# Block-sparse attention with a following MLP: v cast on chip, masks turned by DMA, narrower bounds and a new order

## The chip, the cores and the metric

The kernel runs on one core of one Trainium2 chip. The metric is the device time in microseconds (us) of one execution, as the median of several runs of the same kernel. A profiled execution of its own gives the page and the trace that are shown; times in the profile count from the start of its span.

The names of the engines are those of the profile: PE is TensorE, PEld its weight loads, DVE is VectorE, ACT is ScalarE, POOL is GpSimd, SP is SyncE. SP here only issues DMAs. SBUF is the on-chip memory, PSUM the memory into which TensorE writes.

## The reference

There are two stages. q, k and v are fp32 of shape (4, 8, 768, 64): batch, head, position, feature. The first stage is an attention in which each query sees six chunks of 32 keys:

```
ub[s, c] = sum over d of max(q[s,d] * kmin[c,d], q[s,d] * kmax[c,d])     # kmin, kmax: over the 32 keys of chunk c
ub = where(s // 32 >= c, ub, -1e9)
chosen[s] = the 6 chunks with the largest ub[s, :]
scores = q @ k.T / 8, masked to the chosen chunks and to keys t <= s
x = softmax(scores) @ v
```

The heads are then put side by side, which gives x of shape (4, 768, 512), and the second stage is a normalised two-layer MLP with a residual:

```
xn = (x - mean(x)) / sqrt(var(x) + 1e-6) * g_ln
out = x + relu(xn @ w_ch1) @ w_ch2       # 512 -> 2048 -> 512, fp32 out
```

## The kernel before

**Tiling.** A tile has 128 positions, so a sequence has 6 tiles, in two halves of 3 (r = 0 and r = 1). Two heads go together, since two times 64 features fill 128 partitions: a group g is one batch and one pair of heads. There are 16 groups, four to a batch. Groups 0 to 3 (batch 0) are loaded and prepared in two halves, groups 4 to 15 whole.

**Steps of a group.** `ld` and `ldb` load k and q by SP's DMA queue. `turn` brings features onto partitions: on PE through PSUM for groups 0 to 3 (L218, fp32), on DVE in blocks of 32 x 32 for the others (L212). `kbound` reduces k to the minimum and maximum of each chunk (L262, L263), and `kdiag` spreads these into a block matrix (`BD`, and its two 16-bit parts `BH`). With the identity max(qm, qM) = qm + relu(q)(M - m), the upper bounds are matrix products. In groups 0 to 3 `qpos` makes two fp32 operands on ACT and `bounds` runs L309 and L313; six products that nobody reads, 240 columns wide (L306), stand ahead of them. In the other groups `qhi`, `qlo` and `qrel` split q into 16-bit parts, and `bounds` takes 20 products of 96 columns (L297): four for each of five tiles. (The first tile needs no choice.) `select` (L326 to L332, on DVE) adds the causal term, takes the 8 largest of each row and writes a row of ones where a chunk is not chosen (`MN`).

**The mask in the scores.** The operands of the score products have 128 rows, of which only 64 are features of one head. The other 64 rows carry the mask: on the side of k constant rows with -61440 where a key belongs to a chunk (`rrows`, L148 and L149, copied from a constant `RT`), on the side of q the turned `MN`. `maskt` turns it on PE (L341), and `mring` copies it from PSUM into the operands `QA` and `QB` with two DVE copies (L346, L347). `qring` brings q there and `kcopy` k (L268, L269, ACT). A product of both then gives the score with the mask in it.

**Attention.** `smm` takes the score products of up to four blocks for each of the two heads (L396) into a PSUM tile, `sexp` is the exponential on ACT (L404), `diag` clears the part above the diagonal on POOL (L411), `values` multiplies by v with a column of ones beside it (L423), and `norm` divides by that column's sum (DVE, L437). `pstat` takes statistics of x (L453).

**v.** `ldv` loads v by POOL's DMA queue, which turns fp32 into fp16 on the way (L189, L196).

**MLP.** For each batch and half: `centre` (L465, DVE), `xt` (L482, three DMA transposes on SP's queue), `m1` (L489) and `relu` (L498, ACT) in eight pairs of hidden tiles, `m2` (L511), `fin` (L520, DVE: scale, add x, store by SP). `rstd` gives the reciprocal deviation (L476, POOL). `w1` and `w2` load the weights in four pieces each, on POOL's queue; each first copies one element of `kc` into the piece (L155, L159), so that a load cannot start before that `kc` exists.

**The order.** Each engine works through its own queue in order. The order is written out: the string `ORDER` lists the steps, and the instructions of each engine, SP's and POOL's DMA issues among them, are chained as the steps come in the string. A step such as `m1.0.0.8` is batch 0, half 0, hidden tiles 8 and 9. PSUM has two pools: two tiles of two banks (tag `mm`: scores and m1) and four of one bank (tag `one`: turns, bounds, masks, values, m2). A step that takes a tile waits until the user before the last two, or the last four, is done with it. `warm` and `idle` (L357) are products that nobody reads; they keep PE occupied.

Of the kernel before, what the change touches and what calls it, by code (L numbers as in the profile page):

```python
# [9 lines left out]
ACTF = mybir.ActivationFunctionType  # L10
ALU = mybir.AluOpType
# [8 lines left out]
def kernel(  # L20
# [10 lines left out]
    nc = tc.nc  # L31
# [9 lines left out]
    VW = 72  # L41
# [36 lines left out]
    RT = const.tile([P, S], F16, name="RT", tag="RT")  # L78
    tiny = const.tile([1, 1], F32, name="tiny", tag="tiny")
    hsel = const.tile([P, 3, 2], F32, name="hsel", tag="hsel")  # L80
# [18 lines left out]
    st = [dict() for _ in range(NG)]  # L99
    hf = {}  # L100
    x_tiles = {}

    def consts():
        make_identity(nc, ident_f)
        rr = RT[0:64, :]
        nc.gpsimd.memset(rr, -NEGM)
        nc.gpsimd.affine_select(
            out=rr, in_=rr, compare_op=ALU.is_ge, fill=0.0,  # L110
            base=0, pattern=[[1, S]], channel_multiplier=-CH,
        )
        nc.gpsimd.affine_select(
            out=rr, in_=rr, compare_op=ALU.is_ge, fill=0.0,
            base=CH - 1, pattern=[[-1, S]], channel_multiplier=CH,
        )
# [7 lines left out]
        nc.vector.memset(hsel[0:64, 0, 1:2], -KS)  # L124
        nc.vector.memset(hsel[64:P, 0, 0:1], -KS)
        nc.vector.memset(hsel[0:64, 1:3, 1:2], KS)
        nc.vector.memset(hsel[64:P, 1:3, 0:1], KS)
# [18 lines left out]
    def rrows(i, r):  # L146
        c = slice(r * TR * P, (r + 1) * TR * P)
        nc.vector.tensor_copy(KA[i][64:P, c], RT[0:64, c])  # L148
        nc.vector.tensor_copy(KB[i][0:64, c], RT[0:64, c])  # L149

    def w1(j, g):
        c = slice(j * HID // 4, (j + 1) * HID // 4)
        nc.gpsimd.tensor_copy(w1b[0:1, 0, c.start:c.start + 1], st[g]["kc"][0:1, 0, 0:1])  # L155
        nc.gpsimd.dma_start(w1b[:, :, c], w1_r[:, :, c])

    def w2(j, g):
        nc.gpsimd.tensor_copy(w2b[0:1, 4 * j, 0:1], st[g]["kc"][0:1, 0, NCH // 2:NCH // 2 + 1])  # L159
        nc.gpsimd.dma_start(w2b[:, 4 * j:4 * j + 4, :], w2_r[:, 4 * j:4 * j + 4, :])  # L160

    def ld(g, i):
        b, hp = divmod(g, HP)
        both = ldp.tile([P, 2, TR, 2, D], F32, name="raw", tag="raw")
        for e, (nm, src) in enumerate((("kn", k), ("qn", q))):
            t = st[g][nm, i] = both[:, e]
            for hh in range(2):
                nc.sync.dma_start(
# [13 lines left out]
    def ldv(g, i=None):  # L182
        b, hp = divmod(g, HP)
        if not i:
            st[g]["va"] = vap.tile([P, 2, NT, VW], F16, name="va", tag="va")
            nc.gpsimd.memset(st[g]["va"][:, :, :, D:D + 1], 1.0)
        va = st[g]["va"]
        if i is None:
            nc.gpsimd.dma_start(  # L189
                va[:, :, :, 0:D].rearrange("p h t d -> p (h t) d"),  # L190
                v[b, 2 * hp:2 * hp + 2].rearrange("h (t p) d -> p (h t) d", p=P),
            )
            return
# [469 lines left out]
```

## Time and profile before

| | us |
|---|---|
| median of three runs (282.27, 282.9, 287.85) | 282.9 |
| profiled execution | 284.41 |
| its span | 282.5 |
| PE busy (2529 products) | 268.8, 95% |
| DVE busy (627 instructions) | 209.9, 74% |
| ACT busy (246) | 185.0, 65% |
| POOL busy (162) | 92.4, 33% |

The page counts as busy what an engine computes; issuing a DMA is not counted for SP, and for POOL the casting DMAs of v and of the weights appear as instructions in the timeline. PE's busy time is drawn from modelled ends, so a busy PE may still run slowly or stretched by waits. A slice is 282.5/40 = 7.06 us long. In a line of a group the columns are: line, engine, operation, out<-in, partitions x elements and type, count, busy us, mean ns. In the chain a line is start, duration and what it was.

### The profile page before, as it was taken

To read this page: it belongs to the slowest core of one execution; us is meant where nothing else is said; L and a number is where in the kernel's file an instruction comes from. 1 tells how busy PE (TensorE), PEld (TensorE's weight loads), DVE (VectorE), ACT (ScalarE), POOL (GpSimd) and SP (SyncE) were. 2 spreads that over 40 slices of the span, in tenths; PEclk is the share of its full clock that TensorE was granted. 3 is DMA by queue.
4 is the path that set the end of the run, shared out by engine and by line. 5 is a ranking of instruction groups with operands and counts; after the bars stand their busy time and mean duration, and the time that the engine had idled before them with its cause. 6 is when DMAs were issued, how large, how long until landed. Compare 5 with 4: busy or idle time off the path is not lost.

```text
span 282.5 us, 6594 instructions
## 1 busy us (share of the span) xinstructions
PE 268.8 (95%) x2529; PEld 177.8 (63%) x2529; DVE 209.9 (74%) x627; ACT 185.0 (65%) x246; POOL 92.4 (33%) x162
## 2 busy tenths in 40 slices
PE   5899699999998999999999999999999999999994
PEld 2788567677655867666666766576667745555541
DVE  6889969999999979997779899969885842301112
ACT  2889969999946867867677776776968332423320
POOL 8816335453391022607462702410254000100100
PEclk9599979999999999999999999999999999999999
DMA  6999999999999764698997667663021120500202
GB/s 140 206 192 146 212 144 138 169 166 194 151 155 182 129 141 95 89 157 164 115 142 149 127 63 83 113 117 111 0 67 39 39 56 15 152 2 37 74 2 111
DMA packets 136062, 32.41 MB, mean 115 GB/s; under 512 B 127072, under 2 KB 132960, under 8 KB 136032
## 3 DMA queue, kind: packets, MB, share of 16 engines
q1 hardware_dynamic: 106640, 24.39, 45.0%
q0 software_dynamic: 29248, 7.34, 27.5%
q8 instruction: 20, 0.33, 0.5%
q10 hardware_dynamic: 144, 0.26, 0.4%
q14 instruction: 10, 0.08, 0.1%
HBM read 27.53 MB, written 6.29 MB: 120 GB/s over the span
## 4 chain that ended last, share of the span: by engine, by line
PE 82%; DVE 6%; DMA 5%; ACT 4%; issue 1%; SPq 0%; DVEq 0%; ACTq 0%
PE yp L511 28%; PE mm L489 27%; PE mm L396 12%; PE sm L423 6%; DMA raw<-in_k_dram 4%; PE ub L297 3%; ACT pt L404 2%; PE ub L313 2%; PE tr L218 2%; PE trh L341 1%; PE idle L357 1%; DMA raw<-in_q_dram 1%; PE ub L306 1%; DVE kc L262 1%; DVE kc L263 1%
## 5 line engine op out<-in xcount | busy, mean ns | idle before, releaser
L404 ACT ACTIVATE pt<-mm 128x1024 f16<-128x1024 f32 (+2 forms) x96 | 84.5, 916 | 20.4 <-PE mm L396 19.5
L511 PE MATMUL yp<-w2b,hT 128*128 128x512 f16 (+2 forms) x400 | 92.5, 370 | 0.0
L489 PE MATMUL mm<-xT,w1b 128*128 128x384 f16 x512 | 87.8, 326 | 1.3 <-ACT hT L498 1.2
L498 ACT ACTIVATE hT<-mm 128x768 f16<-128x768 f32 x64 | 51.3, 810 | 54.1 <-PE mm L489 53.7
L489 PEld LDWEIGHTS <-w1b 128*128 128x128 f16 x512 | 49.4, 98 | 34.5 <-issue 1.6
L511 PEld LDWEIGHTS <-hT 128*128 128x128 f16 x400 | 37.5, 98 | 34.1
L411 POOL TENSOR_SCALAR_AFFINE_SELECT pt<-pt 128x768 f16<-128x768 f16 x32 | 28.1, 885 | 77.4 <-ACT pt L404 77.3
L520 DVE SCALAR_TENSOR_TENSOR ot<-yp,rstd,x 128x512 f32<-128x512 f32 (+2 forms) x25 | 17.8, 716 | 44.5 <-PE yp L511 34.8
L396 PE MATMUL mm<-QA,KA 128*128 128x128 f16 (+2 forms) x224 | 34.2, 246 | 1.4 <-ACT pt L404 0.8
L396 PE MATMUL mm<-QB,KB 128*128 128x128 f16 (+2 forms) x224 | 34.2, 246 | 0.0
L476 POOL TENSOR_TENSOR rstd<-ve,mhalf 128x3 f32<-128x3 f32 x8 | 7.0, 873 | 58.0 <-DVE ve L473 57.9
L423 PE MATMUL sm<-va,pt 128*128 128x65 f16 x672 | 25.3, 193 | 0.6 <-ACT pt L404 0.3
L423 PEld LDWEIGHTS <-pt 128*128 128x128 f16 x672 | 24.0, 98 | 2.5 <-ACT pt L404 0.4
L396 PEld LDWEIGHTS <-KA 128*128 128x128 f16 x224 | 18.1, 98 | 11.2 <-issue 2.9
L453 DVE BATCH_NORM_STATS2 bst<-x 128x6 f32<-128x128 f32 x96 | 20.3, 278 | 0.0
L396 PEld LDWEIGHTS <-KB 128*128 128x128 f16 x224 | 17.9, 98 | 3.9 <-issue 0.4
L438 DVE TENSOR_TENSOR x<-sm,rden 128x384 f32<-128x384 f32 x32 | 17.8, 557 | 1.1
L465 DVE SCALAR_TENSOR_TENSOR xc<-x,mv,gall 128x512 f16<-128x512 f32 x24 | 16.8, 756 | 0.6 <-DMA xT<-xc 0.6
L281 POOL TENSOR_TENSOR kc<-kc 128x24 f32<-128x24 f32 x12 | 6.0, 502 | 31.3 <-DVE kc L263 21.7
L346 DVE COPY QA<-trh 64x640 f16<-64x640 f16 (+2 forms) x20 | 8.6, 428 | 8.3 <-PE trh L341 7.9
L218 PE MATMUL tr<-ident_f,raw 128*128 128x128 f32 x48 | 8.9, 316 | 4.2 <-DMA raw<-in_q_dram 2.2
L189 POOL DMA_DIRECT2D va<-in_v_dram x12 | 12.7, 1060 | 0.1
(85 smaller groups left out, 347.7 us busy)
## 6 DMA issues: line engine op xcount, KB each, us to landing
out_dram<-ot SPq DMA_DIRECT2D x23, 256.0 KB, 2.1
qnb<-in_q_dram SPq DMA_DIRECT2D x48, 96.0 KB, 3.2
knb<-in_k_dram SPq DMA_DIRECT2D x48, 96.0 KB, 3.3
va<-in_v_dram POOLq DMA_DIRECT2D x12, 192.0 KB, 5.4
w1b<-in_moe_w_ch_dram POOLq DMA_DIRECT2D x4, 512.0 KB, 8.2
w2b<-in_moe_w_ch_dram POOLq DMA_DIRECT2D x4, 512.0 KB, 7.1
raw<-in_k_dram SPq DMA_DIRECT2D x16, 96.0 KB, 4.3
raw<-in_q_dram SPq DMA_DIRECT2D x16, 96.0 KB, 4.2
```

What stands on the lines that cost most here:

```text
L218: nc.tensor.transpose(pst[:, t * P:(t + 1) * P], src[:, t], ident_f)
L396: nc.tensor.matmul(sc[:, hh, o:o + w * P], ks[:, t * P:(t + 1) * P], qs[:, s * P:(s + w) * P], start=True, stop=True,)
L404: nc.scalar.activation(st[g]["pt", r][:, 4 * i:4 * i + o].rearrange("p n h x -> p h n x"), st[g]["sc", r, i][:, :, 0:o * P].rearrange("p h ...
L411: nc.gpsimd.affine_select(out=dv, in_=dv, compare_op=ALU.is_ge, fill=0.0, base=0, pattern=[[0, 2 * TR], [1, P]], channel_multiplier=-1,)
L423: nc.tensor.matmul(pv[:, hh, s2, :], pt[:, where[t, s], hh, :], va[:, hh, t, 0:D + 1], start=(t == 0), stop=(t == s),)
L438: nc.vector.tensor_tensor(xh(b, r)[:, :, 2 * hp:2 * hp + 2, :].rearrange("p s h d -> p h s d"), pv[:, :, :, 0:D], rden.to_broadcast([P, 2, ...
L453: nc.vector.bn_stats(half(b, r)["st"][:, i, hp], xh(b, r)[:, i, 2 * hp:2 * hp + 2].rearrange("p h d -> p (h d)"),)
L465: nc.vector.scalar_tensor_tensor(h["xc"][:, i, :], xs, h["mv"][:, i, 0:1], gall, op0=ALU.subtract, op1=ALU.mult,)
L489: nc.tensor.matmul(hp_[:, i, 0:TR * P], w1b[:, kt, (m + i) * P:(m + i + 1) * P], h["xT"][:, kt], start=(kt == 0), stop=(kt == KT1 - 1),)
L498: nc.scalar.activation(h["hT"][:, m:m + 2], h["hp", m][:, :, 0:TR * P], ACTF.Relu, scale=HS)
L511: nc.tensor.matmul(h["yp", i][:, cs], h["hT"][:, kt, i * P:(i + 1) * P], w2b[:, kt, cs], start=(kt == 0), stop=(kt == KT2 - 1),)
L520: nc.vector.scalar_tensor_tensor(ot[:, cs], h["yp", i][:, cs], h["rstd"][:, i:i + 1], xh(b, r)[:, i].rearrange("p h d -> p (h d)")[:, cs], ...
```

## The change

- **v.** `ldv` loads fp32 by SP's queue into a buffer `vr` (two of them), and a new step `vcast` copies it as fp16 into `va`: on POOL (22 of 32 steps), ACT (5) or DVE (5). SP gets 40 DMAs for it.
- **Masks of groups 4 to 15.** `maskt` is a DMA transpose on SP's queue, from SBUF to SBUF, into one buffer; `mring` copies from there, on POOL (8) or DVE (4).
- **Bounds of groups 4 to 15.** Three of the four products of a tile take only the chunks that the tile can see: 32, 48, 64, 80 or 96 columns.
- **First x.** For batch 0, half 0, `xt` turns on PE (12 products), and a new step `xe` copies the result from PSUM.
- **Start.** q of groups 0 and 1 is loaded by ACT's queue; k of group 1 and of group 0 come first, and the load of g_ln (`gall`) comes after them. `RT` is gone: `rrows` multiplies a broadcast part of the identity by -61440. In groups 0 to 3 a new step `qcopy` makes one scaled fp32 copy of q (`q32`), from which `qpos` makes `r32` and `qring` the rows of `QA` and `QB`; `kdiag` takes the difference of maximum and minimum there too.
- **Weights.** The copies of one element are gone; w1.0, w1.1, w1.2, w1.3 and then the four pieces of w2 stand in `ORDER` after `vcast.1.1`, `vcast.2.1`, `diag.0.1` and `qring.3.1`.
- **Engines.** A step may be written `step@n`: n picks the engine from a list. So `kcopy` of the later groups is 11 times on POOL, `relu` 11 times on DVE, `qhi` 7 times on DVE, `norm` 5 times on ACT, `rrows` 3 times on ACT, `kdiag` of groups 0 to 3 6 times on POOL.
- **Fill products.** For steps on PE, n picks how many unread products stand ahead (`busy`): 8 to 32 of 122 or 128 columns, 4 to 16 of 240, 2 to 8 of 512. The six ahead of `bounds` and the separate `idle` steps are gone.
- **Order.** `ORDER` is another string from its first step to near its last.

The diff's core (`ORDER` only by its places around the weights):

```diff
+    fill = {P: (8, 16, 32), 240: (4, 8, 16), 512: (2, 4, 8), 122: (8, 16, 32)}
+    def pick(*engines):
+        return engines[min(other[0], len(engines) - 1)]
...
     def rrows(i, r):
-        nc.vector.tensor_copy(KA[i][64:P, c], RT[0:64, c])
-        nc.vector.tensor_copy(KB[i][0:64, c], RT[0:64, c])
+        for t, o in ((KA[i], 64), (KB[i], 0)):
+            scaled(
+                pick(nc.vector, nc.scalar),
+                t[o:o + 64, r * TR * P:(r + 1) * TR * P].rearrange("p (c e) -> p c e", e=CH),
+                ident_f[o:o + 64, o + c.start:o + c.stop].unsqueeze(2).to_broadcast([64, n, CH]), -NEGM,
+            )
...
-    def w1(j, g):
+    def w1(j):
         c = slice(j * HID // 4, (j + 1) * HID // 4)
-        nc.gpsimd.tensor_copy(w1b[0:1, 0, c.start:c.start + 1], st[g]["kc"][0:1, 0, 0:1])
         nc.gpsimd.dma_start(w1b[:, :, c], w1_r[:, :, c])
...
+            queue = nc.scalar if (i, nm) == (0, "qn") and g < 2 else nc.sync
...
-    def ldv(g, i=None):
-            nc.gpsimd.dma_start(
-                va[:, :, :, 0:D].rearrange("p h t d -> p (h t) d"),
-                v[b, 2 * hp:2 * hp + 2].rearrange("h (t p) d -> p (h t) d", p=P),
-            )
+    def ldv(g, i):
+        t = st[g]["vr", i] = ldp.tile([P, NT, D], F32, name="vr", tag="vr", bufs=2)
+        if g >= HP:
+            nc.sync.dma_start(t, v[b, 2 * hp + i].rearrange("(t p) d -> p t d", p=P))
+            return
...
+    def vcast(g, i):
+        eng = pick(nc.gpsimd, nc.scalar, nc.vector)
+        if g >= HP:
+            copy(eng, va[:, i, :, 0:D], t)
...
+    def busy(o, n=None):
+        w = o.shape[1]
+        for _ in range((0, *fill[w])[other[0]] if n is None else n):
+            nc.tensor.matmul(o, MN[0][:, 0, :], MN[0].rearrange("p s c -> p (s c)")[:, 0:w], start=True, stop=True)
...
     def kcopy(g, i=None):
-        nc.scalar.copy(KA[g % NK][0:64, a * P:z * P], kt[0:64, :])
-        nc.scalar.copy(KB[g % NK][64:P, a * P:z * P], kt[64:P, :])
+        eng = pick(nc.scalar, nc.vector) if g < HP else pick(nc.scalar, nc.gpsimd, nc.vector)
+        copy(eng, KA[g % NK][0:64, a * P:z * P], kt[0:64, :])
+        copy(eng, KB[g % NK][64:P, a * P:z * P], kt[64:P, :])
...
     def bounds(...):
+                    w = NCH if e == 0 else (s + 1) * P // CH
                     nc.tensor.matmul(
-                        ub[:, s - 1].rearrange("p l h c -> p (l h c)"), st[g][nm][:, s * P:(s + 1) * P],
-                        BH[g % NB][:, arr].rearrange("p l h c -> p (l h c)"), start=(e == 0), stop=(e == 3),
+                        ub[:, s - 1, :, :, 0:w], st[g][nm][:, s * P:(s + 1) * P],
+                        BH[g % NB][:, arr, :, :, 0:w], start=(e == 0), stop=(e == 3),
                     )
...
     def maskt(g, i=None):
+        if g >= HP:
+            pm = prp.tile([P, NT - 1, P], F16, name="mT", tag="mT", bufs=1)
+            nc.sync.dma_start_transpose(pm, st[g]["mn"].rearrange("p s c -> p (s c)"))
+            return
...
     def xt(b, r, i):
+        if (b, r) == (0, 0):
+            pst = h["xp", i] = ps_t.tile([P, KT1, P], F16, name="xtr", tag="one")
+            for kt in range(KT1):
+                nc.tensor.transpose(pst[:, kt], h["xc"][:, i, kt * P:(kt + 1) * P], ident_h)
+            return
...
     ORDER
-        ... sexp.2.0.0 w1.2.3 w1.1.3 w1.0.2 ld.3.1 ...
+        ... vcast.1.1 ldv.2.1 w1.0 vcast.2.1 ...
+        ... xe.0.0.0 w1.1 ldv.3.1 ... qring.4 w1.2 w1.3 kdiag.3.1@1 ...
+        ... m1.0.0.0 turn.5.qn turn.5.kn relu.0.0.0@1 w2.2 ... m1.0.0.2 w2.0 ... w2.3 rrows.2.1@1 w2.1 ...
```

## The prediction

> **What bounds the kernel now.** I read the page's slices first, then ten-microsecond windows, the chain of waits, a stretch of the timeline and the groups by shape. Slices:
>
> ```profile
> PE   5899699999998999999999999999999999999994
> DVE  6889969999999979997779899969885842301112
> PEclk9599979999999999999999999999999999999999
> ```
>
> PE is full from slice 14 (92 us) to the end; its gaps and the two drops of the clock (5 and 7) lie in the first 40 us. Windows (time; busy and count of PE, PEld, DVE, ACT, POOL; clock; DMA; GB/s):
>
> ```profile
> 0.00:10.00 10.00, 5.99 (x24) 3.23 (x25) 7.12 (x29) 4.33 (x9) 9.12 (x22) 0.91 0.90 157
> 10.00:20.00 10.00, 9.61 (x72) 8.63 (x70) 7.84 (x33) 8.12 (x20) 2.94 (x4) 0.75 1.56 210
> ...
> 80.00:90.00 10.00, 8.82 (x55) 4.91 (x54) 9.96 (x12) 5.08 (x7) 6.13 (x12) 1.00 1.46 178
> ...
> 100.00:110.00 10.00, 10.00 (x126) 7.01 (x125) 7.70 (x23) 8.02 (x10) 3.42 (x4) 1.00 0.60 125
> ```
>
> DVE's nine windows before 90 us are busy 7.12, 7.84, 9.38, 8.97, 8.68, 9.80, 9.69, 9.85 and 9.96: 8.7 us short, 5.0 of it before 20 us. At 100 us that has turned: PE 10.00, DVE 7.70. The chain has the same hand-over:
>
> ```profile
> 0.80 4.78 DMA raw<-in_k_dram
> ...
> 29.83 5.59 DMA raw<-in_k_dram
> 36.43 2.13 PE idle L357 x5
> ...
> 80.23 1.50 DVE q L235
> 83.08 1.48 DVE r L242
> ...
> 120.34 11.72 PE mm L489 x72
> ```
>
> A k load waits at the start and another at 30 us; DVE ends last around 80 us; after 92 us only PE does. L235 and L242 cost 1.5 us there. The timeline of DVE and POOL tells why:
>
> ```profile
> 80.12 0.92 POOL L411 TENSOR_SCALAR_AFFINE_SELECT pt<-pt 128x768 f16<-128x768 f16 x1
> 80.23 1.50 DVE L235 SCALAR_TENSOR_TENSOR q<-qnT,q 128x640 f16<-128x640 f32 x1
> 81.66 1.50 DVE L241 TENSOR_SCALAR r<-q 128x640 f16<-128x640 f16 x1
> ```
>
> L241 takes 0.31 us where POOL is idle. L332, L235, L241 and L242 lose 3.3 us in that stretch, some 6.5 in the whole head.
>
> So the span is a sum: DVE's work up to the hand-over, DVE's idle time and latencies, PE's work after it, the tail. Before: DVE's instructions ahead of fin.0.0.1, for whose PSUM slot bounds.7 waits, come to 80.7 us; idle 8.7; semaphores and the first product 1.9; PE's own work is 252.7 in all (below), 65.7 of it ahead of bounds.7, so 187.0 remains; after the last matmul (278.4) 4.1. Together 282.4, and the span is 282.5.
>
> PE's own work takes rates from the chain where PE isn't waiting: 512 columns 216 ns (0.86 for 4), 384 columns 162 (1.30 for 8), 96 columns 42.5 (0.85 for 20), 65 columns 30.3 (0.91 for 30), 128 columns 56 (0.45 for 8). Times counts: m2 83.0 (368 of 512, 16 of 384 and 16 of 128 columns), m1 83.2 (512), scores 37.0 (448 of three widths), values 20.4 (672), bounds 10.2 (240), masks 4.5 (80), the turns and bounds of batch 0 14.1, small ones 0.3.
>
> **What the Trainium skill says.** "SBUF — State Buffer", Who interferes with whom: VectorE and GpSimd share an SBUF port pair under an exclusive lock. The trace agrees (1.50 against 0.31 us, above). "DMA: Bandwidth & Descriptors", SWDGE vs HWDGE vs iDMA: a cast within a DMA needs the GpSimd queue, so v on SP must be fp32 and cast afterwards. The trace has the old form alone. "TensorE: Matmul & The Clock Gate", Part 1: The HAM clock gate: too little work halves TensorE's clock. It agrees: clock 0.75 in 10 to 20 us, and a fill of 512 columns takes 426 ns there, 216 later.
>
> **The change part by part.**
>
> *PE.* Masks: 60 of 80 turns go, ×56 ns = −3.4. Narrower bounds: three of four products of a tile drop from 96 columns to 32, 48, 64, 80, 96; by the 65-column rate the first three cost 30 and the fourth 36, so a group saves 3×(3×12.2+6.5) = 0.13 us, and twelve 1.5; between 0 and 2.4 if a narrow product costs no less, or falls in proportion. I take 2.0. First x on PE: 12×56 = +0.7. Total 248.0. Fills grow from 33 to 114 products, 9.6 us; they stand ahead of products that wait, so I cost them at nothing. Where nothing waits, each is PE time, 2 to 3 us if a quarter is misplaced.
>
> *DVE up to the hand-over.* The same tally over the new order says values.5.1, which waits for the slot of select.7, hands over: one select more than before. Less: rrows 3 of 8 on ACT and cheaper −2.8, later mask copies on POOL or at SBUF price −2.4, early ones on ACT −2.0, kdiag −0.8, constants −0.5. More: the extra select 2.2, kcopy 2×0.93, relu 2×0.86 (L498's tile, priced as the reduce of 768 fp32), qhi 3×0.5 ("VectorE: DVE Perf Modes", The perf-mode tier table: fp32 from SBUF runs at 2×; 0.86 if it doesn't), qrel 1.2, qlo 0.8, xT copies 2×0.43, qring 0.6, pstat 0.6, qpos 0.5, norm 0.2. Net +3.6: 84.3. By then PE has done 70.7; 177.5 remain. The extra select costs 2.2 but moves 5 us of PE work before the hand-over.
>
> *DVE idle.* The first k and q: the 256 KB of gall no longer ahead, q on ACT's queue: about 1 us earlier. The wait at 30 us: ld.3.1's issue on SP took 3.86 us beside three 512 KB weight loads and landed 5.6 later; now it precedes them: 1.5 less. Idle 6.2, latency 1.9.
>
> *POOL and the lock.* Up to the hand-over POOL's computing goes from 26.8 to about 50 us. By the slope between a CAST of 96 elements (264 ns) and an affine of 768 (865): vcast 9×0.52 = 4.7, kcopy 4×2×0.87 = 7.0, mring 2×2×0.75 = 3.0, qring 4×2×0.52 = 4.2, kdiag some 4.4. POOL loses in exchange the issue of v (1.0 us a piece). The lock cost 6.5 us for 26.8 of POOL's, but only where a fast DVE form meets it; selects, reduces, transposes and statistics show no effect. In proportion +6, at nothing 0; I take 2 and keep −1 (fewer DMA writes by POOL) to +6.
>
> *v, masks and SP's queue.* SP gets 40 v DMAs and 12 mask transposes, loses 3 xT and 4 q. At 0.53 us (median issue) and 1.2 (xT) that is +32 us on 155; SP was issuing 19 of each 20 us at first, so ldb, xt and qring behind it are late by what it waits. Those are issued two groups ahead. A later mask is now SP 1.2, landing 2.5, POOL 1.5 in place of PE 0.28, DVE 0.98: some 4 us longer; by PE's tally its scores stand over 5 us further on, so I cost it at nothing; without that distance it is up to 4 us once, since later ones overlap. With one mT buffer a maskt also waits on SP for the mring before it, and behind it stand ldb, xt, qring and the stores; xt is what PE's m1 waits for. On POOL a vcast waits for v's landing (3 to 4 us), and behind it stand diag, for which values waits, kdiag and the weights. Both are covered while PE has other work ahead; DVE's idle term would grow otherwise.
>
> *Weights.* Without the artificial wait eight 512 KB loads run back to back on POOL's queue, 3.3 us apart as the three before (28.3, 31.2, 34.8). I place w1.0's issue at 36 and the columns that m1.0.0.8 needs at 49, where PE wants them at 47.6; such a wait of up to 3.5 us is absorbed, since DVE hands over later. ACT gives up relus and copies and stays under its tally.
>
> **Sum.** 84.3 + 6.2 + 1.9 + 2.0 + 177.5 + 4.1 = 276.0 against the span of 282.5. The profiled execution is 284.4 (1.9 around the span), 1.5 above the median of 282.9; I carry the difference of −6.5 to the median: 276.4.
>
> **Rivals.**
>
> *The lock takes it.* POOL's work coincides with qlo, qrel and the selects as at 80 us: 6 to 7 instead of 2, 281. For: 23 us more work. Against: much of it falls on unaffected operations.
>
> *PE becomes the bound sooner.* DVE's idle falls by 3 and the lock by 2 below my terms: 271. For: fills keep the clock up and ACT takes DVE's copies. Against: DVE's idle of before was mostly loads, which the change only brings forward by 2.5.
>
> *Weights late (slower).* PE is in order: while m1.0.0.8 waits, nothing behind it runs. The span is then 276.0 + (landing − 47.6 − 3.5); it passes that of before once the third w1 piece lands after 57.6. For: the burst shares DMA with SP's new v loads, and a w1 piece took 8.2 us from issue to landing in the median. If pieces come one after another at that, w1.0 lands at 43 and the third at 59.4: 284.3, in the median 284.7. Against: three overlapped before.
>
> *The change isn't what it says.* v stays fp32 in HBM, so the same bytes are read and twice as many written on the chip; if the DMA engines bind in the head (their column reads 1.56 at 10 to 20 us), moving v to another queue brings nothing and costs the casts. The loads would then land no earlier, idle would stay at 8.7, and the sum is 278.5, within the first case.
>
> **Numbers.** As summed: 0.57 (273.5 to 279). Lock: 0.20 (279 to 283). PE sooner: 0.13 (269 to 273.5). Late weights or SP: 0.10 (283 to 291). Leaving out the ends, 270 to 284. Two per cent, which is about what a measurement of this kernel can tell, is 277.2 and 288.6: of the first case 0.43, with 0.13, is faster: 0.56; slower 0.05; the rest within.
>
> **What would show it.** DVE at 9.7 or more up to about 95 us; the last DVE piece of the chain near 94; chain pieces of 20 products of L297's successor near 0.7 us instead of 0.85; no `trh` of 640 columns; L411 and the new POOL casts beside 1.5-us DVE instructions if the lock counts; no gap ahead of m1.0.0.8. I am wrong if PE has a gap at L489 in the first batch, if SP's queue holds xt or qring, or if PE's last gap comes before 85 us.

## The result, and the profile after

The changed kernel takes 286.62 us in the median (four runs, 286.13 to 287.56); the kernel before takes 283.25 us in the median of its four runs (282.27 to 287.85). Executions more than 1.5% above the fastest of the same kernel, such as the one of 287.85, count as slow and are left out of every ratio given here. The ratio is 1.0134, with a 95% interval of 1.0086 to 1.0182: 1.3% slower, where 2.3% faster was forecast (276.4 us, range 270 to 284). How much slower is less certain than that interval says, since only three executions of the kernel before stand in it: measured again beside the experiments below, its median was 285.06 to 286.1 us, and 286.62 is 0.2 to 0.6% above that. No measurement shows a gain. The profiled execution took 286.18 us and its span is 284.5 us, 2.0 more than before.

The slices of the page, as shown for the kernel before:

```profile
PE   5899988996999999999999999999999999999994
DVE  7686999889799997999999899969964685321412
PEclk9856999999999999999999999999999999999999
```

PE is full from slice 11 on, as before from slice 14, but the half clock has moved: it now lies at 14 to 28 us, where PE had its full clock before. The windows (time; busy and count of PE, PEld, DVE, ACT, POOL; clock; share of the DMA engines; GB/s):

```profile
0.00:10.00 10.00, 6.80 (x46) 4.21 (x46) 7.41 (x29) 3.94 (x7) 1.51 (x9) 1.00 0.86 184
10.00:20.00 10.00, 8.99 (x53) 8.04 (x53) 6.89 (x24) 7.72 (x18) 5.52 (x17) 0.60 0.82 169
20.00:30.00 10.00, 10.00 (x103) 9.24 (x104) 6.97 (x26) 6.71 (x13) 2.73 (x8) 0.72 0.96 185
...
50.00:60.00 10.00, 9.78 (x65) 5.75 (x62) 8.68 (x28) 6.15 (x9) 3.23 (x6) 1.00 1.43 216
60.00:70.00 10.00, 7.51 (x130) 6.13 (x128) 8.75 (x27) 5.65 (x7) 4.33 (x7) 1.00 1.32 193
70.00:80.00 10.00, 10.00 (x102) 6.23 (x99) 8.36 (x23) 7.72 (x18) 6.79 (x10) 1.00 0.91 159
80.00:90.00 10.00, 10.00 (x94) 6.24 (x93) 9.90 (x23) 6.31 (x9) 5.07 (x10) 1.00 0.65 161
```

DVE is short of 30 by 8.7 us in the first three (5.7 before) and short of 30 by 4.2 between 50 and 80 us (0.7 before); between 30 and 50 us it gains, with 0.4 idle in place of 2.4. PE reads 10.00 at 20 to 30 us although its clock is 0.72 and 42 of its 103 products there are fills: a full PE column is not a working PE. What DVE waited for up to 105 us (engine, line, releaser: us in total, times, longest):

```profile
DVE QA L106 <- PE trh L367: 2.5, 1, 2.5
DVE hT L545 <- PE mm L535: 2.2, 2, 1.3
DVE kc L284 <- PE tr L234: 2.1, 4, 0.9
DVE kc L284 <- ACT KB L106: 2.0, 1, 2.0
DVE rden L467 <- PE sm L453: 1.5, 1, 1.5
```

and in the kernel before:

```profile
DVE QA L346 <- PE trh L341: 3.0, 2, 1.9
DVE m L331 <- PE ub L313: 2.1, 2, 1.9
DVE kc L262 <- PE tr L218: 1.1, 2, 0.7
```

DVE waited for turned masks (`QA`) and for turned k (`kc`) before as well, 3.0 us for the masks. Three of the five are new: `hT L545` is `relu` on DVE, which waits for PE's m1; `kc` waits for a PSUM tile that ACT has to clear; and `rden` at 75.6 us is norm.3.1, which waits for values.3.1. In exchange `m L331`, the selects' wait for the bounds, is gone. The waits that the two lists name add up to 8.1 us before and 11.2 after. The chain of waits, in its stretch up to 130 us (start, duration, what):

```profile
24.23 1.64 PE tr L222 x16
...
41.84 11.15 DMA w1b<-in_moe_w_ch_dram
53.04 7.99 PE mm L535 x48
61.05 0.96 DVE hT L545
...
94.02 0.66 DVE ot L569
...
99.21 0.85 PE ub L322 x20
...
101.42 4.61 DMA vr<-in_v_dram
```

L222 is `busy`, the fill products: the line shown has 16 of them, and 68 of the 114 are on the chain. A piece of w1 that lands at 53.0 is on it, then PE's m1, then the `relu` on DVE, then mostly DVE to 97 us, then PE. From 101.4 to 110.1 us it runs through a load of v and POOL's casts and copies behind it. PE is busy for 9.84 of the ten us from 100 on, so that stretch costs little.

### Where the time went

The sum of the prediction can be read off any trace. I take the end of select.7 on DVE as the hand-over in both kernels (the prediction named fin.0.0.1 for the kernel before and select.7 for the changed one), DVE's busy and idle time up to it, and what PE still has to do by its own rates at that moment (fills not counted).

| us | before | after | difference |
|---|---|---|---|
| DVE busy to the end of select.7 | 86.7 | 88.7 | +2.0 |
| DVE idle to there | 8.9 | 13.7 | +4.8 |
| select.7 ends | 95.6 | 102.4 | +6.8 |
| PE's own work left (252.7 − 69.9, 248.0 − 71.2) | 182.8 | 176.8 | −6.0 |
| lost on PE after that | 0.0 | 1.2 | +1.2 |
| last matmul ends | 278.4 | 280.4 | +2.0 |

Of PE's −6.0, 4.7 is work that the change took away, and 1.3 stands earlier in the order. DVE's idle time takes 4.8 of it back, DVE's work 2.0. PE's lost time (elapsed minus own work) is 25.7 us before and 32.4 after; fills keep PE busy for 11.1 us of it before and 15.5 after.

This table says where the time stands, not what caused it: work plus idle time is the end of select.7 by definition, and DVE's idle time is in large part waiting for PE, which at other places waits for DVE. The causes have to come from the experiments.

### The profile page after: what moved, and what is told of

Read it like the earlier page. It is cut to its first block, busy times and chain, and to the rows that moved or that the text cites. A ratio compares the mean times of both kernels' runs of the same rounds, so it can differ in the third digit from the quotient of the medians.

```text
span 284.5 us, 6773 instructions
## 1 busy us (share of the span) xinstructions
PE 270.4 (95%) x2554; PEld 179.2 (63%) x2554; DVE 218.7 (77%) x621; ACT 162.1 (57%) x238; POOL 113.7 (40%) x203
## 4 chain that ended last, share of the span: by engine, by line
PE 72%; DVE 10%; DMA 9%; POOL 3%; ACT 3%; issue 1%; SPq 1%; DVEq 0%; ACTq 0%; POOLq 0%
PE yp L560 25%; PE mm L535 25%; PE mm L422 9%; PE sm L453 6%; DMA w1b<-in_moe_w_ch_dram 4%; DMA vr<-in_v_dram 2%; PE ub L322 2%; DMA raw<-in_k_dram 2%; PE ub L335 2%; PE tr L222 1%; ACT pt L430 1%; DVE ot L569 1%; DMA raw<-in_q_dram 1%; DVE kc L285 1%; DVE kc L284 1%
## 5 line engine op out<-in xcount | busy, mean ns | idle before, releaser
L547 ACT ACTIVATE hT<-mm 128x768 f16<-128x768 f32 x53 | 43.0, 811 | 72.3 <-PE mm L535 72.3
L437 POOL TENSOR_SCALAR_AFFINE_SELECT pt<-pt 128x768 f16<-128x768 f16 x32 | 29.1, 918 | 17.9 <-ACT pt L430 17.8
L453 PE MATMUL sm<-va,pt 128*128 128x65 f16 x672 | 26.4, 193 | 0.4 <-ACT QB L106 0.3
L453 PEld LDWEIGHTS <-pt 128*128 128x128 f16 x672 | 24.7, 97 | 2.7 <-issue 0.4
L545 DVE TENSOR_SCALAR hT<-mm 128x768 f16<-128x768 f32 x11 | 10.5, 957 | 18.9 <-PE mm L535 18.9
L106 POOL CAST va<-vr 128x384 f16<-128x384 f32 x22 | 12.1, 551 | 27.3 <-DMA vr<-in_v_dram 27.1
L500 DVE SCALAR_TENSOR_TENSOR xc<-x,mv,gall 128x512 f16<-128x512 f32 x24 | 18.4, 821 | 2.6 <-DMA xT<-xc 2.6
L106 POOL COPY QA<-mT 64x640 f16<-64x640 f16 x8 | 6.1, 768 | 28.4 <-DMA mT<-MN 28.4
L474 DVE TENSOR_TENSOR x<-sm,rden 128x384 f32<-128x384 f32 x27 | 15.0, 557 | 0.9
L222 PEld LDWEIGHTS <-MN 128*128 128x128 f16 x114 | 9.1, 112 | 7.6 <-DVE MN L353 2.7
## 6 DMA issues: line engine op xcount, KB each, us to landing
w1b<-in_moe_w_ch_dram POOLq DMA_DIRECT2D x4, 512.0 KB, 10.6
w2b<-in_moe_w_ch_dram POOLq DMA_DIRECT2D x4, 512.0 KB, 13.8
```

The lines of the kernel that those rows point to most:

```text
L106: return eng.copy(o, i) if eng is nc.scalar else eng.tensor_copy(o, i)
L437: nc.gpsimd.affine_select(out=dv, in_=dv, compare_op=ALU.is_ge, fill=0.0, base=0, pattern=[[0, 2 * TR], [1, P]], channel_multiplier=-1,)
L453: nc.tensor.matmul(pv[:, hh, s2, :], pt[:, where[t, s], hh, :], va[:, hh, t, 0:D + 1], start=(t == 0), stop=(t == s),)
L474: nc.vector.tensor_tensor(o.rearrange("p s h d -> p h s d"), pv[:, :, :, 0:D], rden.to_broadcast([P, 2, TR, D]), ALU.mult,)
L500: nc.vector.scalar_tensor_tensor(h["xc"][:, i, :], xs, h["mv"][:, i, 0:1], gall, op0=ALU.subtract, op1=ALU.mult,)
L547: nc.scalar.activation(h["hT"][:, m:m + 2], h["hp", m][:, :, 0:TR * P], ACTF.Relu, scale=HS)
```

## The experiments

Runs whose name begins with a_ are edits of the changed kernel, those with b_ of the kernel before. Each ratio is to the kernel before as measured beside that run. That kernel's own median ranged from 283.25 to 286.1 from one such measurement to the next, so a comparison is safest between runs that were measured together. The changed kernel itself was measured once, beside the lowest of these medians.

### Parts of the change on the kernel before

```diff
 b_narrow, in bounds:
-    ub[:, s - 1].rearrange("p l h c -> p (l h c)"), ..., BH[g % NB][:, arr].rearrange(...)
+    w = NCH if e == 0 else (s + 1) * P // CH
+    ub[:, s - 1, :, :, 0:w], ..., BH[g % NB][:, arr, :, :, 0:w]
 b_mask_dma, in maskt:
+    if g >= HP:
+        pm = prp.tile([P, NT - 1, P], F16, name="mT", tag="mT", bufs=1)
+        nc.sync.dma_start_transpose(pm, st[g]["mn"].rearrange("p s c -> p (s c)"))
```

> The kernel before with the narrower bounds alone (32 to 96 columns in place of 96 for three of four products). My term: 12 groups at 0.13 to 0.2 us, the span falls from 282.5 by 1.5 to 2.0, since nine of twelve groups lie after 90 us, where PE sets the time. Rival: narrow products cost no less than wide ones, no difference.

Measured: ratio 0.9952 (0.9909 to 0.9995), span 280.4. PE's lost time is 25.7, what it was before, and its own work, counted by the products' rates, 2.0 less. The term of the prediction holds (the span fell by 2.1; the ratio gives 0.5%, about 1.4 us), and this kernel is the fastest full one here, ahead of both.

> The kernel before with the later masks turned by DMA alone, in the same places of its order, copied by DVE from SBUF. My term: 60 PE turns of 56 ns go (3.4 us of PE time, 2.5 of it after the hand-over to PE), and DVE copies fall by 0.4 us for each group ahead of it: span 278 to 280. Rival L (latency): its order has the copies close behind the turns, DVE waits some 4 us for each of the first masks, and SP holds the next loads behind them: 283 to 287.

Measured: ratio 1.0624 (1.0549 to 1.0699), span 301.2: the rival, and four times its size (18.7 us more, where its range ended at 4.5). DVE's list of waits up to 140 us begins with

```profile
DVE QA L351 <- DMA mT<-MN: 17.4, 4, 8.6
```

so the first four masks cost 17.4 us of DVE. Their transposes were issued far apart, at 66.3, 95.7, 112.4 and 120.8 us, and landed 8.9, 4.9, 2.6 and 4.1 us later. In this order the copies stand right behind the turns. In the changed order the masks' copies stand further on, and there DVE's list has no such line; POOL waits for masks instead, and is not on the chain for it before 106 us. The same part costs 18.7 us in one order and shows no cost to DVE in the other, so no price can be put on it without the order.

### Weights

```diff
 a_w1_early (and a_w_spread, a_w_as_before in the same manner, with the w2 pieces moved too), in ORDER:
-  vcast.1.1 w1.0 vcast.2.1 w1.1 ... diag.0.1 w1.2 w1.3
+  diag.0.0 w1.0 ... kdiag.1.1@1 w1.2 ... vcast.1.0 w1.1 ... diag.1.0 w1.3
 b_w_burst:
-  w1.2.3 w1.1.3 w1.0.2 ... w1.3.3 ... w2.0.0 ... w2.1.0 ... w2.2.1 ... w2.3.1      (each with its copy from kc)
+  w1.0 w1.1 w1.2 w1.3 w2.0 w2.2 w2.1 w2.3      (in a row where w1.3.3 stood, no copies)
```

> The changed kernel with the four pieces of w1 issued earlier on POOL's queue (after diag.0.0, kdiag.1.1, vcast.1.0 and diag.1.0, so from 26 us on in place of 39) and the piece that m1.0.0.8 needs second. Theory W: PE's wait for that piece (it lands at 53.0 us) goes, lost PE time between 40 and 55 us falls from 3.1 to about 1, span 282 to 283. Rival D: DVE sets the end of the head, the 2 us come back at a later wait: 284 to 285. Rival L: the weights delay ld.3.1 and ldb as before the change, and lost time before 40 us grows: 285 or more.

Measured: 1.0459 (1.0369 to 1.055), span 293.8: rival L. The piece that m1.0.0.8 needs lands at 36.9 in place of 53.0, but a load of q that SP issues at 28.2 lands at 38.3, ld.3.1's two loads of k at 40.8 and 43.7; PE has lost 32.4 us by 60 us (25.6 in the changed kernel). Most of that growth lies at 40 to 60 us, not before 40 as rival L had it (23.1 against 22.4 there).

> The changed kernel with the eight weight loads spread on POOL's queue: w1.0, w1.2, w1.1, w1.3 after diag.1.0, diag.3.0, diag.2.0, diag.0.1 (about 30, 34, 38 and 42 us in place of 39 to 43), w2.0 to w2.3 after qring.3.1, diag.1.1, kdiag.5, diag.2.1 (about 48, 51, 60, 64 in place of 48 to 50). Theory B (burst): the eight loads back to back hold up SP's queue from 40 to 68 us (a q load issued at 43 lands 17.7 us later, a mask 11.3), DVE and PE wait for what SP loads; spread, SP's loads land within 8 us, DVE idles less than 1.5 us between 50 and 80 us in place of 4.2, lost PE time after 40 us falls from 10 to 5 us, span 279 to 281. Theory W (only the wait of m1.0.0.8 counts): 282 to 283. Rival D (DVE's work sets the end): 284 to 285.

Measured: 1.0308 (1.0196 to 1.042), span 290.3: none of the three. DVE idles 16.5 us up to select.7.

> The changed kernel with the weight loads where the kernel before issues them by its profile: three w1 pieces at about 22 us, the fourth at 35, the w2 pieces at 48, 58, 61, 65. Theory B: no load of SP lands later than 12 us after its issue beyond 40 us, but ld.2.1 and ld.3.1 are held up at 22 to 33 us; lost PE time grows by 2 to 3 before 40 us and falls by 5 after it: span 281 to 284. If weights don't matter: 284 to 285.

Measured: 1.0422 (1.0316 to 1.0528), span 293.6, outside both. With v on SP too, three pieces of w1 at 23 to 25 us cost more here than in the kernel before: PE has lost 31.4 us by 60 us.

> The kernel before (span 282.5 us) with the weight loads as a burst: no copies from kc, and all eight in a row where w1.3 stood (about 35 us). Theory B: SP's loads issued after 36 us land 10 to 18 us late, PE's lost time between 40 and 100 us grows from 4.5 by 5 to 8, while that before 40 us shrinks by up to 3 since ld.3.1 no longer waits at 26 us: span 285 to 289. If a burst doesn't matter, only the gain at ld.3.1 is left: 279.5 to 282.5.

Measured: 1.036 (1.0278 to 1.0442), span 294.0, 11.5 more than before and above the 285 to 289 of theory B. Windows of it:

```profile
40.00:50.00 10.00, 3.59 (x55) 3.19 (x53) 9.88 (x25) 5.09 (x8) 5.46 (x10) 0.90 1.25 183
50.00:60.00 10.00, 6.40 (x29) 3.28 (x30) 0.37 (x1) 2.48 (x4) 0.78 (x1) 0.58 1.37 210
```

DVE is idle for 9.6 us of the second one; in all it waits 14.9 us there for one load of q. Whether the burst of the changed kernel costs anything there was open after these four; small weights tell it:

```diff
 a_w_quarter, b_w_quarter:
-  w1b[:, :, c], w2b[:, 4 * j:4 * j + 4, :]                     (loads)
+  w1b[:, :, c.start:c.start + P], w2b[:, 4 * j:4 * j + 1, :]
-  w1b[:, kt, (m + i) * P:(m + i + 1) * P], w2b[:, kt, cs]      (products)
+  w1b[:, kt, (m + i) // 4 * 4 * P:((m + i) // 4 * 4 + 1) * P], w2b[:, kt // 4 * 4, cs]
```

> The changed kernel with a quarter of the weights: each piece loads 128 of its 512 columns (w1) or one of its four rows of tiles (w2), and the products read that quarter four times, so the same instructions run on other numbers and three quarters of the weights are left out. Theory T (weight traffic): the weight loads, back to back from 39 to 68 us, are what holds m1 and SP's loads; DVE's idle before select.7 falls from 13.7 to 8 to 10, PE's lost time from 32.4 to 26 to 28, span 278 to 280. Rival E (early part): the order, fills and low clock before 40 us set it; span 282.5 or more.

> The kernel before with the same quarter of the weights. Its m1 doesn't wait for weights, but ld.3.1 waits at 26 to 35 us beside three of them. Theory T: a gain of 1 to 3, span 279.5 to 281.5, less than in the changed kernel, so the two end within 1.5 us of each other or the changed one first (its PE work is 4.7 us less). Rival E: the changed kernel stays behind by 2 or more.

Measured: the changed kernel 1.0134 (1.0047 to 1.0221), span 286.6; the kernel before 0.9867 (0.9798 to 0.9935), span 279.6. The changed kernel gained nothing and stays 7.0 us behind, which is what rival E forecast; that the early part of the order sets its time, as E puts it, isn't shown by this run. The kernel before did gain, 2.9 us of span, as theory T had it for that kernel; part of this may be the clock, which was 1.00 in each of its first four windows (0.91, 0.75, 1.00 and 0.83 before). The loads did become short. The DMA part of the changed kernel with a quarter (KB, median us from issue to landing; 10.6 and 13.8 with whole weights):

```profile
w1b<-in_moe_w_ch_dram POOLq DMA_DIRECT2D x4, 128.0 KB, 5.9
w2b<-in_moe_w_ch_dram POOLq DMA_DIRECT2D x4, 128.0 KB, 3.8
```

and its windows:

```profile
50.00:60.00 10.00, 10.00 (x80) 6.33 (x79) 8.94 (x29) 5.94 (x8) 2.49 (x5) 1.00 0.66 114
60.00:70.00 10.00, 7.52 (x122) 6.03 (x120) 8.89 (x27) 5.90 (x7) 6.97 (x10) 1.00 0.70 118
70.00:80.00 10.00, 10.00 (x110) 6.38 (x107) 7.14 (x24) 7.43 (x18) 4.60 (x8) 1.00 0.58 75
```

The last column falls from 216 to 114 GB/s at 50 to 60 us, and DVE, idle 4.2 us between 50 and 80 us with whole weights, is idle 5.0. PE's lost time at 40, 60, 80 and 100 us is 23.0, 25.9, 30.4 and 31.5 (22.4, 25.6, 30.2 and 31.2 with whole weights). So the weight that lands at 53.0 is on the chain, and it is not what sets the time: with it at 48.3 the DVE `relu` waits as long (1.8 against 2.2).

### v

```diff
 a_v_late:    -vcast.0.1@1                +vcast.0.1                      (POOL in place of ACT)
 a_v_pool, in ldv (vcast does nothing):
-  nc.sync.dma_start(t, v[b, 2 * hp + i]...)
+  nc.gpsimd.dma_start(va[:, i, :, 0:D], v[b, 2 * hp + i]...)
 a_v_actq, in ldv:
-  nc.sync.dma_start
+  nc.scalar.dma_start
```

> The changed kernel with vcast.0.1 on POOL in place of ACT. Theory V: ACT waits there 0.86 us for the load of v and casts 0.51, and turns, copies and DVE behind it stand still (DVE idle 1.97 us at 12.5); without it the span falls by 1 to 1.5, to 283 to 283.5. Rival S: the order of loads on SP's queue sets the pace up to 30 us (ld.1.1 lands at 20.9, ld.2.1 at 24.2), and the span changes by less than 0.5.

Measured: 1.0205 (1.0096 to 1.0314), span 288.1. The wait `kc L284 <- ACT KB` falls from 2.0 to 0.6, as theory V has it, but another follows 1 us later (1.5, `m L352 <- PE ub L335`), and POOL, with 0.5 us more to do, then issues the weights 3.8 us later (42.6 against 38.8). No gain, and neither forecast: the span lies above both.

> The changed kernel with v as before: cast within the DMA, on POOL's queue, issued at the places where the changed kernel issues it on SP; no vcast. Theory Q (SP's queue): by 40 us SP issues 17 loads of v at about 0.5 us each, and k and q stand behind them; without them k and q come up to 8 us sooner, DVE's idle before 30 us falls from 8.7 to 5 to 6 and lost PE time at 30 us from 19.4 to 15 to 17; the weights on POOL's queue come sooner too; span 279 to 282. Rival M (memory traffic): what the DMA engines move in the head is the same and the loads only collide elsewhere; span 284 to 286.

Measured: the four executions spread from 289.54 to 297.61, too far for a ratio (the lowest of the kernel before beside them is 282.38). The fastest is the profiled one, with a span of 287.8, above the range of Q and of M. Lost PE time by 20 us is 12.6 (13.9), so SP's queue does give something back, but by 40 us it is 22.4 in both. POOL's own order now holds v: after the first four loads (2.1 to 4.6 us) the next is issued at 12.6 us, and w1.0 at 41.5 in place of 38.8.

> The changed kernel with the fp32 loads of v issued by ACT's queue in place of SP's; casts stay. Theory Q: SP is free of v as in the kernel with v on POOL, at about 0.5 us of ACT's time a load (ACT is not at its limit after 20 us): span 280 to 283. Rival M: 284 to 286. Rival A: ACT, which works in order, waits for buffers or issues in front of exponentials: over 286.

Measured: 1.1078 (1.1008 to 1.1149), span 312.0: rival A. In the changed order, v on SP is the best of the three places tried; each of the other two brought delays of its own queue with it, so what SP's loads of v cost by themselves isn't settled.

### Fill products and the `relu` on DVE

```diff
 a_fill_const, in busy (c is 120 for w = 240, else min(w, 128); the first eight fills keep MN[0]):
-  nc.tensor.matmul(o, MN[0][:, 0, :], MN[0].rearrange("p s c -> p (s c)")[:, 0:w], ...)
+  nc.tensor.matmul(o, ident_h, ident_h[:, 0:c].unsqueeze(1).to_broadcast([P, w // c, c]), ...)
 a_no_fill, in ORDER:      -smm.0.0.0@1   +smm.0.0.0      (so for every turn, bounds, smm, values and m1)
 a_relu_act, in ORDER:     -relu.0.0.0@1 ... relu.0.0.14@1   +relu.0.0.0 ... relu.0.0.14
```

The fill products read a mask tile, MN[0], which select.5 writes. PE's list of waits for the changed kernel has the line

```profile
PE sm L222 <- DVE MN L353: 2.5, 1, 2.5
```

which is 16 fills ahead of values.2.1 waiting for a result that nobody needs there.

> The changed kernel (span 284.5 us, median 286.6) with one edit: its fill products read the constant identity in place of the mask tile MN[0]. Theory F: select.5 writes MN[0], and the 16 fills ahead of values.2.1 read it, so PE waits for DVE there (2.5 us by the list of waits at 65 to 68 us, 3.7 us of lost PE time in that window). With a constant the wait goes and the span falls by 2.5 to 3.5, to 281 to 282. Rival D (DVE sets the end of the head): PE only reaches the next wait for DVE sooner, the loss comes back at a later step by 100 us, and the span changes by less than 1.

Measured: 1.0068 (1.0031 to 1.0106), span 285.0. The wait is gone, and so is DVE's wait `rden`; lost PE time at 70 us falls from 30.1 to 28.1. At 90 us it is 30.2 against 30.4. By the traces that is rival D: select.7 ends at 101.7 in place of 102.4, and 0.7 is all there is; the span is 0.5 longer.

> The changed kernel without all fill products but the first eight. Theory F: they cost PE time and a wait and bring nothing that is needed: 18.3 us of PE's time up to 95 us goes to fills, 13.4 without the first eight, of which some lie in waits; span 278 to 282. Rival C (clock): the fills keep TensorE at full clock, and without them the clock stays low longer than the slices 2 to 4 (14 to 28 us) of the changed kernel; span 285 to 288.

Measured: 1.0062 (1.0032 to 1.0093), span 285.5. Windows:

```profile
20.00:30.00 10.00, 9.09 (x87) 8.39 (x86) 8.88 (x30) 7.96 (x16) 4.68 (x11) 0.81 0.87 169
...
50.00:60.00 10.00, 7.93 (x39) 4.19 (x38) 7.98 (x27) 4.11 (x7) 3.84 (x7) 0.83 1.43 216
60.00:70.00 10.00, 9.47 (x137) 7.13 (x135) 6.49 (x20) 7.45 (x10) 4.10 (x6) 1.00 1.32 197
```

At 20 to 30 us the clock is higher without fills (0.81 against 0.72) and DVE does 1.9 us more, against rival C. At 50 to 60 us, where PE waits for weights, it is lower without them (0.83 against 1.00), as rival C would have it, and the span lies in that rival's range; so C is right in its number and in one of the two stretches. In the changed kernel the timeline shows what the fills do there:

```profile
24.03 1.85 PE L222 MATMUL tr<-MN 128*128 128x128 f16 x16
26.05 0.27 PE L367 MATMUL trh<-ident_h,MN 128*128 128x128 f16 x2
26.36 0.29 DVE L106 COPY QA<-trh 64x256 f16<-64x256 f16 x1 [2.49 <-PE trh L367]
```

Sixteen products at half clock, 1.85 us, stand ahead of the mask turn for which DVE has been idle 2.49 us. Without fills that wait is 0.4. But what is gained by 40 us (lost time 20.8 against 22.4) is given back from 50 us on: DVE's list now begins with

```profile
DVE hT L545 <- PE mm L535: 5.2, 2, 4.8
```

DVE stands 4.8 us in front of relu.0.0.14, behind PE's m1. So the next edit takes the relus off DVE.

> The changed kernel (span 284.5 us; DVE idle 13.7 and busy 88.7 up to the end of select.7 at 102.4) with the two relus of batch 0, half 0 that it puts on DVE (relu.0.0.0 and relu.0.0.14) back on ACT. Theory R (coupling): DVE, whose work sets the end of the head, stands idle 2.2 us at these two since PE's m1 waits for weights, and computes 1.9 us in them; on ACT both go, DVE idle falls to 10 to 11.5, select.7 ends 3 to 4 us sooner, span 280.5 to 282. Rival F (PE): select.7 isn't what sets the end, PE's lost time comes from weights and fills, and the span changes by less than 1.

Measured: 1.0234 (1.0181 to 1.0287), span 288.7: neither. The waits at `hT` are gone, DVE's work is 2.0 less (86.7), and its idle time is 19.5 in place of 13.7:

```profile
DVE rden L467 <- PE sm L453: 5.0, 3, 3.1
DVE QA L106 <- PE trh L367: 4.1, 2, 2.4
DVE ubm L347 <- PE ub L322: 2.5, 1, 2.5
```

DVE came sooner to the next results of PE, which come no sooner. The wait has moved, and why it also grew isn't settled (the clock at 70 to 80 us was 0.83 here and 1.00 in the changed kernel). With less work DVE ended later: in this order DVE's own work alone does not set the end of select.7.

> As that, and no fill products but the first eight. Without fills alone DVE idled 4.8 us at relu.0.0.14 (58.5 to 63.4 us), which ate what the missing fills had saved. Theory R: idle before select.7 falls from 12.6 to 6 to 8, span 277 to 280. Rival F: 283 to 286.

Measured: 1.0082 (1.0047 to 1.0117): rival F, no better than no fills alone.

> The changed kernel with these two relus and the two copies of the turned x (xe) on ACT, w1.2, which m1.0.0.8 needs, ahead of w1.1, and the w2 pieces in the order of their use, two after qring.3.1, one after kdiag.5 and one after diag.2.1. Theory R with weights: 0 to 2 below the kernel with the relus alone, 279.5 to 282: the wait of m1.0.0.8 is 2.7 shorter, but it no longer holds DVE. Rival B (burst): SP's loads land sooner, 278 to 279.5.

Measured: 1.0207 (1.0163 to 1.0251), span 292.1, DVE idle 20.6: neither.

> The same without fill products but the first eight. Theory R: 276 to 279, DVE idle before select.7 below 7 us. Rival: the clock drops without fills and takes it back, 280 to 283.

Measured: 1.0089 (1.005 to 1.0128), span 284.7. DVE's work to select.7 is 85.9, the least of the changed kernel's variants, and its idle time 15.5. The span lies above both forecasts.

> The spread loads, and no fill products but the first eight. Without fills alone the changed kernel had lost 1.6 us less by 40 us and gave it back by the wait for weights at 50 to 60 us. Theory B: with the weights spread the gain stays: 1.5 below the spread kernel, 277.5 to 280. Theory D: the same span as the spread kernel.

Measured: 1.008 (1.0044 to 1.0117), span 286.7, DVE idle 15.3: 3.6 below the spread kernel, more than either forecast, but not down to 280.

These pairs differ in the fills (in the second row the fills read a constant):

| | with fills | without |
|---|---|---|
| the changed kernel | 1.0134 (1.0086 to 1.0182) | 1.0062 (1.0032 to 1.0093) |
| the same, a_fill_const | 1.0068 (1.0031 to 1.0106) | 1.0062 (1.0032 to 1.0093) |
| weights spread | 1.0308 (1.0196 to 1.042) | 1.008 (1.0044 to 1.0117) |
| relus on ACT | 1.0234 (1.0181 to 1.0287) | 1.0082 (1.0047 to 1.0117) |
| relus, xe on ACT, weights reordered | 1.0207 (1.0163 to 1.0251) | 1.0089 (1.005 to 1.0128) |

In the last three rows both kernels of a pair were measured together, and the intervals lie apart: there the fills cost 2.3, 1.5 and 1.2%. For the changed kernel itself no cost is shown. The two of the first row were not measured together, their intervals overlap, and the profiled spans say the opposite (284.5 with, 285.5 without); the two of the second row were, and differ by 0.06%.

### What all of them have in common

| us | DVE work | DVE idle | select.7 ends | PE work left | lost after | last matmul |
|---|---|---|---|---|---|---|
| before | 86.7 | 8.9 | 95.6 | 182.8 | 0.0 | 278.4 |
| b_narrow | 87.3 | 7.4 | 94.7 | 181.5 | 0.2 | 276.4 |
| b_w_quarter | 86.7 | 6.0 | 92.7 | 182.8 | 0.0 | 275.5 |
| b_w_burst | 86.5 | 20.6 | 107.1 | 182.8 | 0.1 | 290.0 |
| after | 88.7 | 13.7 | 102.4 | 176.8 | 1.2 | 280.4 |
| a_fill_const | 88.9 | 12.8 | 101.7 | 176.8 | 2.5 | 281.0 |
| a_no_fill | 90.4 | 12.6 | 103.0 | 176.8 | 1.6 | 281.4 |
| a_w_quarter | 87.4 | 15.3 | 102.7 | 176.8 | 3.1 | 282.6 |
| a_v_pool | 91.6 | 14.8 | 106.4 | 176.5 | 0.8 | 283.7 |
| a_relu_act | 86.7 | 19.5 | 106.3 | 176.8 | 1.5 | 284.6 |
| a_w_spread | 90.4 | 16.5 | 106.9 | 176.9 | 2.4 | 286.2 |
| a_w1_early | 88.3 | 22.6 | 110.9 | 176.8 | 2.1 | 289.8 |

The span follows the end of select.7 in all of these; only a_v_actq (15.3 lost after it) and b_mask_dma (8.1) lose much later too. DVE's work is 86 to 92 in these rows, and what differs is its idle time. In no edit of the changed order does it come below 12.6, and in the old order with its weights light it is 6.0.

The half clock at 14 to 28 us is no explanation either, as far as the executions show. Of twenty executions of a_fill_const, two had a mean clock of 0.991 and 0.992 and took 287.36 and 287.35 us (median 286.91); one of a_no_fill had 0.994 and took 286.58 (median 286.5). The changed kernel's own four had 0.976. In the profile of a_v_pool, mean clock 0.994, DVE is idle for 14.8 us all the same.

What stays open: which property of the new order holds DVE's idle time above 12 us. Shown is that it is not the traffic of the weights (a quarter of them, no gain), and not the fills or the two relus alone; moving v off SP's queue did not lower it either (14.8 and more). Fills and light weights together weren't tried; without fills DVE waits longest just where PE waits for weights, so they may hide each other.

## Why the prediction was wrong

**The form of the sum holds.** Span = DVE's work + its idle time up to the hand-over, + PE's work after it, + the tail. The sum said 276.0, the span is 284.5. By its terms: 92.5 for the end of select.7 (84.3 + 6.2 + 2.0) is 102.4, 9.9 more; the 1.9 of latency is 1.2 (what is lost after select.7); 177.5 for PE's remaining work is 176.8; the tail 4.1 is 4.1.

**The failed step is "DVE idle".** The prediction took 8.7 us and subtracted what the change does for two loads: "about 1 us earlier", "1.5 less. Idle 6.2". It is 13.7, so 7.5 of the 9.9 stand here. The loads did come sooner (the first turn starts at 6.35 in place of 8.5; ld.3.1's loads land by 33.8 in place of 36.4). But idle time is not a list of loads from which entries can be struck out. DVE, PE and ACT wait for each other in a written order, and with another order there are other waits: 2.5 for a mask behind 16 fills (masks had 3.0 before), 2.0 for a PSUM tile that ACT clears after waiting for v, 2.2 for m1 at the new `relu` on DVE, 1.5 for values.3.1, which PE reaches late after fills that waited for DVE itself. The `relu` was counted as 2×0.86 of DVE's work; that DVE, the bound, thereby comes to wait for PE was not looked at. Yet taking away one of these waits (a_fill_const, a_v_late, a_relu_act) did not shorten the span: another took its place. So the list says where the idle time stands; why the new order has more of it stays open.

**"Fills ... I cost them at nothing"** rests on too little. They stand ahead of products that wait, but what waits there is often what DVE needs next. In the changed kernel itself no cost of them is shown (1.0068 and 1.0062 when measured together); in three variants of it they cost 1.2 to 2.3%, or 3.4 to 6.5 us, more than the "2 to 3 us if a quarter is misplaced" that stood beside it.

**DVE's work** was 2.4 us too low: 88.7 against 84.3 + 2.0. The three `qhi` took 1.22, 0.56 and 0.85 (0.5 taken), the first of them beside POOL's copies; undisturbed it is 0.55, near the price that was taken. A `relu` measured 0.96 (0.86 taken), and a pair of rrows copies 0.7, up to 1.2 beside POOL.

**The lock** did not grow. Counted against the shortest execution of each form, DVE loses 8.1 us up to select.7, against 8.3 before; 2.0 more was taken. The rival with 6 to 7 more is out.

**The weights.** The third piece landed at 53.0 where 49 was predicted: w1.0 was issued at 38.8, not 36, and the pieces came 2.7 to 4.5 us apart. The rival "weights late" gave 284.7, nearest of all to the 286.6 measured, and its wait is on the chain. It is still not the cause. With the landing at 53.0 that rival's own formula gives 276.0 + 53.0 − 47.6 − 3.5 = 277.9, and a quarter of the weights leaves PE's lost time where it was. The prediction's own words on it, that such a wait is absorbed since DVE hands over later, held.

**Masks, SP's queue.** Costed at nothing by distance: DVE's list shows no wait for them, as predicted. In the old order, without that distance, the price was "up to 4 us once"; the run gave 17.4 over four masks, each issued long after the one before it had landed. Casts on POOL were held to be covered too: POOL waits 18.9 us for loads of v up to 110 us, six times, and how much of that reaches PE no run separates.

**PE's work** −4.7, with 2.0 for the narrower bounds: both as predicted.

**Slips in the working**, none of which changes the outcome: 248.0 − 70.7 leaves 177.3 for PE, not 177.5; SP's +32 us leaves out the four loads of q that go, and with them it is about 30; the fills grow from 41 to 114, since the first eight are in the second number only; and the fill of 512 columns that took 426 ns stands at 36 to 38 us, where the clock drops a second time, not at 10 to 20.

The time ended within 2% of that before, for which 0.39 was given, but on the slower side and 2.6 us above the range: the range covered one wait taking the place of another, not DVE's idle time growing by 4.8 us.

## What to carry to other kernels

Before pricing a new order, list for the engine that bounds which instructions now wait for another engine. Work that is moved onto that engine adds waits for its producer to its own time (here 2.2 us for two relus), but moving it away again need not shorten the wait: with the relus back on ACT, DVE was idle for 19.5 us in place of 13.7.

Idle time of the bounding engine in an old order says little about a new one, and a range should not treat it as a term that can only shrink. A wait on the chain is shown to be a cause only when the time falls with the wait taken away.

Fill products are instructions of an ordered queue: look at what stands behind them and at what they read.

## What the runs showed of the hardware that was not expected

Fill products did not decide the clock by themselves. At 20 to 30 us it is 0.72 with them and 0.81 without; at 50 to 60 us it is 1.00 with them and 0.83 without (the changed kernel and a_no_fill). Nor did a higher mean clock make a_fill_const faster (287.36 us at 0.991, 286.75 at 0.976).

Eight 512 KB loads in a row on POOL's queue delay SP's small loads by many times their length: in the changed kernel a 96 KB load of q, issued at 43.3, lands 17.7 us later, and its issue takes SP 4.4 us (0.5 otherwise). With a quarter of the weights the same load lands 5.9 us after its issue, which takes 2.0. In the old order the burst costs 11.5 us (b_w_burst); in the new one a quarter of the weights brought nothing back.

A product of 32 columns is about as long as one of 48: at full clock both take some 25 ns in the median, 64 columns 29, 80 columns 36 and 96 columns 43, so narrowing stopped paying at about 48.
